# Exact buffer dependencies, earlier loads, and a layer norm spread through the FFN of a transformer block

## The chip, the cores and the metric

The kernel runs on one core of a Trainium2 chip. A core has TensorE (matrix products, with a separate weight load), VectorE, ScalarE and GpSimd, and a sync engine that issues the transfers between HBM and the on-chip memory SBUF. TensorE writes into PSUM, a small memory of eight banks. The metric is the device time of one execution in microseconds (us); lower is better.

## The reference

One pre-norm transformer block on x of 2048 rows by 1024 (bf16), with 32 heads of 32, and an FFN of 3584 hidden columns with the tanh form of GELU:

```python
def _A_ref(x, wqkv, wo):
    qkv = ...                       # (x @ wqkv) split in 3 x 32 heads of 32
    scores = jnp.einsum("bhqd,bhkd->bhqk", q, k) * scale
    p = _softmax(scores, axis=-1)
    o = jnp.einsum("bhqk,bhkd->bhqd", p, v)
    return (...).reshape(B, S, D) @ wo

def _B_ref(x, w1, b1, w2, b2):
    h = _gelu(jnp.einsum("bsd,df->bsf", x, w1) + b1)
    return jnp.einsum("bsf,fd->bsd", h, w2) + b2

h = x + _A_ref(_layernorm(x, axis=-1), A_wqkv, A_wo)
h2 = h + _B_ref(_layernorm(h, axis=-1), B_w1, B_b1, B_w2, B_b2)
```

## The kernel before

**Planner.** The kernel is first written down as a list of tasks for each engine, in program order. Each task names the buffers it reads and writes (`Buf` objects, one per ring slot or bank), and from these the planner derives which semaphore values it must wait for. Each engine then works through its list strictly in order; a wait is issued ahead of the task that needs it (L122). All transfers are issued by the sync engine, also in order (L218), so a transfer whose wait isn't over holds up all later ones.

**Memory.** SBUF and PSUM tensors are allocated like a stack. When a stage ends, its tensors are freed and the next stage's are laid over them. Nothing records which old tensor lies under which new one. So a buffer of a later stage is made by `recycled_buf` (short name `RB`), which lets its first user wait for everything that any engine or transfer lane has been given to do up to then.

**First stage (0 to 247 us).** Layer norm of x, transposes, and the projections to Q, K (transposed) and V, in four chunks of 512 rows.

**Second stage (247 to 1361 us).** Attention. For 4 query chunks x 8 groups of four heads x 16 key tiles, TensorE computes scores (L516), ScalarE the exponentials (L527), TensorE the sums with V (L544) and the denominators (L552). VectorE divides at the end of each group (L563, L564) and writes into OT.

**Third stage (1361 to 1939 us), the one that the change is about.** It works in four chunks (`qc`) of 512 rows, each of four row tiles (`t4`).

- `wo_ln_gen(qc)` is the output projection and the second layer norm. For a row tile it loads the x row tile into `xring3`, makes two accumulation groups of 8 matmuls each (L656) in the PSUM banks `ACC0` onward, copies each out on ScalarE (`attb`, L662) and adds x on VectorE (`hch`, L664). After all four tiles, `ln_batch` takes the statistics of the four (two `bn_stats` a tile, L316, and an aggregate, L318), some small operations on a few columns (L320 to L334, with a square root on ScalarE, L326), then for each tile the subtraction of the mean on ScalarE (L336) and the scaling on VectorE (L339) into `xnb3`. Then each tile is transposed in 8 matmuls (L344) through the one bank `TPB` and copied out on ScalarE into `hnT` (L347).
- `ffn1_gen(qc)` makes the hidden layer in 28 slices (`fc`) of 128 columns, 4 slices for each of 7 blocks of w1 (1 MB each, ring of 3, `w1st`). A slice is 8 matmuls (L701) into one of `NH1P` banks starting at `H1P0`, then the scale and bias on ScalarE (`xh`, L706), two operations on VectorE (`sqf` L709, `uu` L711), and, one slice later, tanh on ScalarE (`th`, L685) and the final product on VectorE (`gT`, L687). `xh`, `sqf`, `uu` and `th` have three slots each.
- `ffn2_plan(qc)` loops over the 28 slices, loads a 256 KB row block of w2 (ring of 4) for each, and adds 8 matmuls (L731), one into each of the eight banks; then come the bias (L737), the residual add on VectorE (`ost`, ring of 4, L746) and the store.

`ffn1_gen` and `wo_ln_gen` are generators. The main loop runs the projection of chunk 0 first. Then, for each chunk, it runs `ffn1_gen(qc)` and after every second slice one step of `wo_ln_gen(qc + 1)`: so the task lists are interleaved in an order fixed by where `yield` stands. Then `ffn2_plan(qc)` follows, which needs all eight banks.

The banks of the third stage before: 0 to 3 for the projection, 4 to 6 for the hidden layer, 7 for the transposes.

Of the kernel before, what the change touches and what calls it, by code (L numbers as in the profile page):

```python
# [6 lines left out]
dt = mybir.dt  # L7
# [43 lines left out]
class Plan:  # L51
    def __init__(self):
        self.tasks = {}
        self.main_flow = {}
        self.all_flows = []

# [4 lines left out]
    def recycled_buf(self):  # L61
        b = Buf()
        for f in self.all_flows:
            hz = f.horizon()
            if hz > 0:
                b.r[f] = hz
        return b
# [61 lines left out]
class LNTemps:  # L129

    def __init__(self, nc, T, pfx, nslots, nbn, mkbuf, tiles=4):
        tq = tiles
        self.stats = T(nc.sbuf_tensor(pfx + "stats", [P, nslots, tq, nbn * 6], dt.float32))
        self.mv = T(nc.sbuf_tensor(pfx + "mv", [P, nslots, tq, 2], dt.float32))
        self.mvb = T(nc.sbuf_tensor(pfx + "mvb", [P, nslots, tq, 2], dt.bfloat16))
        self.mvr = T(nc.sbuf_tensor(pfx + "mvr", [P, nslots, tq, 2], dt.float32))
        self.nm = T(nc.sbuf_tensor(pfx + "nm", [P, nslots, tq, 1], dt.float32))
        self.tb = T(nc.sbuf_tensor(pfx + "tb", [P, nslots, tq, 1], dt.bfloat16))
        self.y0 = T(nc.sbuf_tensor(pfx + "y0", [P, nslots, tq, 1], dt.float32))
        self.r0 = T(nc.sbuf_tensor(pfx + "r0", [P, nslots, tq, 1], dt.float32))  # L140
        self.q0 = T(nc.sbuf_tensor(pfx + "q0", [P, nslots, tq, 1], dt.float32))
        self.y1 = T(nc.sbuf_tensor(pfx + "y1", [P, nslots, tq, 1], dt.float32))
        self.denb = T(nc.sbuf_tensor(pfx + "denb", [P, nslots, tq, 1], dt.bfloat16))
        self.rden = T(nc.sbuf_tensor(pfx + "rden", [P, nslots, tq, 1], dt.float32))
        self.B = [mkbuf() for _ in range(nslots)]
# [15 lines left out]
def build_kernel(nc, A_x, A_wqkv, A_wo, B_w1, B_b1, B_w2, B_b2, out):  # L161
# [23 lines left out]
    with es:  # L185
# [19 lines left out]
        RB = plan.recycled_buf  # L205
# [28 lines left out]
        ident = T(nc.sbuf_tensor("ident", [P, P], dt.bfloat16))  # L234
        ones_pp = T(nc.sbuf_tensor("ones_pp", [P, P], dt.bfloat16))
        ones32 = T(nc.sbuf_tensor("ones32", [P, 32], dt.bfloat16))
        row1 = T(nc.sbuf_tensor("row1", [1, P], dt.bfloat16))
        b2row = T(nc.sbuf_tensor("b2row", [1, D], dt.bfloat16))
        b1col_bf = T(nc.sbuf_tensor("b1col_bf", [P, FC], dt.bfloat16))
        b1half = T(nc.sbuf_tensor("b1half", [P, FC], dt.float32))  # L240
        B_ident, B_ones_pp, B_ones32, B_row1, B_b2row, B_b1bf, B_b1half = (Buf() for _ in range(7))
# [12 lines left out]
        OT = T(nc.sbuf_tensor("OT", [P, NCH, G, 512], dt.bfloat16))  # L254
        B_OT = [[Buf() for _ in range(G)] for _ in range(NCH)]
# [4 lines left out]
        QT = T2(nc.sbuf_tensor("QT", [P, G, S], dt.bfloat16))  # L260
        KT = T2(nc.sbuf_tensor("KT", [P, G, S], dt.bfloat16))
        Vsb = T2(nc.sbuf_tensor("Vsb", [P, NT, D], dt.bfloat16))
        biasm = T2(nc.sbuf_tensor("biasm", [P, G, NCH], dt.float32))
        A2 = T2(nc.sbuf_tensor("A2", [P, G, NCH], dt.float32))
        B2 = T2(nc.sbuf_tensor("B2", [P, G], dt.float32))
        B_QT = [[Buf() for _ in range(NCH)] for _ in range(G)]
        B_KT = [[Buf() for _ in range(NCH)] for _ in range(G)]
        B_V = [[Buf() for _ in range(NVB)] for _ in range(NT)]
        B_biasm = Buf()
        B_A2 = [[Buf() for _ in range(NCH)] for _ in range(G)]  # L270
        B_B2 = [Buf() for _ in range(G)]
# [5 lines left out]
        xnT = T1(nc.sbuf_tensor("xnT", [P, NXT, DC, 512], dt.bfloat16))  # L277
        B_xnT = [[Buf() for _ in range(4)] for _ in range(NXT)]
        NXR = 8
        xring = T1(nc.sbuf_tensor("xring", [P, NXR, D], dt.bfloat16))  # L280
        B_xring = [Buf() for _ in range(NXR)]
        NLN = 8
        NBN = (D + 511) // 512
        xnb = T1(nc.sbuf_tensor("xnb", [P, NLN, D], dt.bfloat16))
        B_xnb = [Buf() for _ in range(NLN)]
        ln1 = LNTemps(nc, T1, "l1", 2, NBN, Buf)
# [3 lines left out]
        wst = T1(nc.sbuf_tensor("wst", [P, NWS, DC, WBLK], dt.bfloat16))  # L290
        B_wst = [Buf() for _ in range(NWS)]
        sqb = T1(nc.sbuf_tensor("sqb", [P, 2, 512], dt.bfloat16))
        B_sqb = [Buf() for _ in range(2)]
        cm = T1(nc.sbuf_tensor("cm", [P, 1], dt.float32))
        B_cm = Buf()
# [3 lines left out]
        tp = ps1.enter_context(nc.psum_tensor("tp", [P, DC * P], dt.bfloat16))  # L299
        B_tp = Buf()  # L300
        NPQ = 3
        psq = ps1.enter_context(nc.psum_tensor("psq", [P, NPQ, 512], dt.float32))
        B_psq = [Buf() for _ in range(NPQ)]
        pn = ps1.enter_context(nc.psum_tensor("pn", [P, 2, 512], dt.float32))
        B_pn = [Buf() for _ in range(2)]
        psv = ps1.enter_context(nc.psum_tensor("psv", [P, 2, 512], dt.float32))
        B_psv = [Buf() for _ in range(2)]

        def ln_batch(L, slot, xs_list, outs_list):
# [25 lines left out]
            for i, ((x_ap, B_x), (xn_ap, B_xn)) in enumerate(zip(xs_list, outs_list)):  # L335
                act(lambda a, L=L, slot=slot, i=i, xn_ap=xn_ap, x_ap=x_ap: a.activation(  # L336
                    xn_ap, x_ap, ACT.Identity, bias=L.nm[:, slot, i, :], scale=1.0),
                    reads=[B_x, Bl], writes=[B_xn])
                dve(lambda v, L=L, slot=slot, i=i, xn_ap=xn_ap: v.tensor_scalar(xn_ap, xn_ap, L.rden[:, slot, i, :], None, ALU.mult),  # L339
                    reads=[B_xn, Bl], writes=[B_xn])  # L340

# [146 lines left out]
        PT = T2b(nc.sbuf_tensor("PT", [P, NPT, 2, 512], dt.bfloat16))  # L488
        B_PT = [RB() for _ in range(NPT)]
        rdenf = T2b(nc.sbuf_tensor("rdenf", [P, 2, 512], dt.float32))  # L490
        B_rdenf = [RB() for _ in range(2)]
# [3 lines left out]
        sT = ps2.enter_context(nc.psum_tensor("sT", [P, NSTP, 2, 512], dt.float32))  # L495
        B_sT = [RB() for _ in range(NSTP)]
        NOD = 2
        OTp = ps2.enter_context(nc.psum_tensor("OTp", [P, NOD, 512], dt.float32))
        DENp = ps2.enter_context(nc.psum_tensor("DENp", [P, NOD, 512], dt.float32))
        B_OTp = [RB() for _ in range(NOD)]  # L500
        B_DENp = [RB() for _ in range(NOD)]

# [84 lines left out]
        Wo = T3(nc.sbuf_tensor("Wo", [P, G, D], dt.bfloat16))  # L587
        B_Wo = RB()
        dma(Wo[:, :, :], A_wo.rearrange("(g p) d -> p g d", p=P), writes=[B_Wo], lanes=lanes_w)
        NHC = 2  # L590
        hch = T3(nc.sbuf_tensor("hch", [P, NHC, 4, D], dt.bfloat16))
        B_hch = [[RB() for _ in range(4)] for _ in range(NHC)]
        attb = T3(nc.sbuf_tensor("attb", [P, 2, OB], dt.bfloat16))
        B_attb = [RB() for _ in range(2)]
        NHN = 2
        hnT = T3(nc.sbuf_tensor("hnT", [P, NHN, DC, 512], dt.bfloat16))
        B_hnT = [[RB() for _ in range(4)] for _ in range(NHN)]
        gT = T3(nc.sbuf_tensor("gT", [P, FC, 512], dt.bfloat16))
        B_gT = [RB() for _ in range(FC)]
        NXR3 = 4  # L600
        xring3 = T3(nc.sbuf_tensor("xring3", [P, NXR3, D], dt.bfloat16))
        B_xring3 = [RB() for _ in range(NXR3)]
        NLN3 = 4
        xnb3 = T3(nc.sbuf_tensor("xnb3", [P, NLN3, D], dt.bfloat16))
        B_xnb3 = [RB() for _ in range(NLN3)]
        ln3 = LNTemps(nc, T3, "l3", 2, NBN, RB)
# [4 lines left out]
        w1st = T3(nc.sbuf_tensor("w1st", [P, NW1, DC, W1B], dt.bfloat16))  # L611
        B_w1st = [RB() for _ in range(NW1)]
        NW2 = 4
        w2st = T3(nc.sbuf_tensor("w2st", [P, NW2, D], dt.bfloat16))
        B_w2st = [RB() for _ in range(NW2)]
        NGL = 3
        xh = T3(nc.sbuf_tensor("xh", [P, NGL, 512], dt.bfloat16))
        sqf = T3(nc.sbuf_tensor("sqf", [P, NGL, 512], dt.bfloat16))
        uu = T3(nc.sbuf_tensor("uu", [P, NGL, 512], dt.bfloat16))
        th = T3(nc.sbuf_tensor("th", [P, NGL, 512], dt.bfloat16))  # L620
        B_xh = [RB() for _ in range(NGL)]
        B_sqf = [RB() for _ in range(NGL)]
        B_uu = [RB() for _ in range(NGL)]
        B_th = [RB() for _ in range(NGL)]
        NOS = 4
        ost = T3(nc.sbuf_tensor("ost", [P, NOS, OB], dt.bfloat16))
        B_ost = [RB() for _ in range(NOS)]
# [4 lines left out]
        B_pb = [RB() for _ in range(8)]  # L632
        ACC0 = 0
        H1P0 = 4
        NH1P = 3
        TPB = 7
        tp3 = pb[:, TPB, :].bitcast(dt.bfloat16)

# [203 lines left out]
```

## Time and profile before

| | |
|---|---|
| time, median of 4 runs | 1942.8 us (1940.69 to 1944.21) |
| span of the profiled execution | 1939.0 us |
| PE (TensorE matmul) busy | 1734.4 us, 89% |
| ACT (ScalarE) busy | 1345.5 us, 69% |
| DVE (VectorE) busy | 507.0 us, 26% |
| third stage | 1360.8 to 1939.0 us |

How to read it: the names in the profile are PE for TensorE's matmuls, PEld for its weight loads, DVE for VectorE, ACT for ScalarE, SPq for the sync engine's queue of transfers. An entry such as `pb<-hnT,w1st` gives the tile written and the tiles read. What stands in brackets at the end of a line is the engine's idle time just before the instruction and what ended it. The shares are averages over three stages with different limits: the second stage, 1114 us long, is mostly ScalarE's, and the third is TensorE's. Two tensors of the first and third stage, `xring` and `xring3`, have one name in the profile, since digits at the end are left out.

### The profile page before, as it was taken

How to read it: one execution, taken by the hardware profiler on the slowest of the kernel's cores; microseconds unless marked ns; L12 is line 12 of the kernel's file. 1: busy time of each engine (PE TensorE's matmuls, PEld its weight loads, DVE VectorE, ACT ScalarE, POOL GpSimd, SP SyncE). 2: the span in 40 equal slices, each digit the busy share in tenths (PEclk: the TensorE clock that was granted, in tenths of full speed). 3: DMA queues.
4: the chain of work that ended last, by engine and by line, in shares of the span. 5: the costliest groups of instructions: out<-in, count | busy, mean ns of one | idle time of the engine just before them, and what ended most of it. 6: DMA issues, size and time to landing. Idle time of an engine off the chain costs nothing.

```text
span 1939.0 us, 24118 instructions
## 1 busy us (share of the span) xinstructions
PE 1734.4 (89%) x9312; PEld 482.7 (25%) x9312; DVE 507.0 (26%) x849; ACT 1345.5 (69%) x1458; POOL 1.0 (0%) x9
## 2 busy tenths in 40 slices
PE   4889989999999999999999999999479779779798
PEld 2344411111111111111111111111134334334343
DVE  5443500010100101001010010110356156165281
ACT  3433389999999999999999999999246045054060
POOL 0000000000000000000000000000000000000000
PEclk9999955555555555555555555555689889889899
DMA  4343200000000000000000000000422432523534
GB/s 113 129 149 122 95 1 1 1 1 1 1 1 1 1 1 1 1 1 1 1 1 1 1 1 1 1 1 1 152 66 76 147 124 93 171 85 109 156 127 131
DMA packets 84176, 100.13 MB, mean 52 GB/s; under 512 B 7265, under 2 KB 64609, under 8 KB 84066
## 3 DMA queue, kind: packets, MB, share of 16 engines
q1 hardware_dynamic: 84066, 98.59, 16.1%
q8 instruction: 78, 1.28, 0.3%
q14 instruction: 32, 0.26, 0.0%
HBM read 94.38 MB, written 4.19 MB: 51 GB/s over the span
## 4 chain that ended last, share of the span: by engine, by line
PE 61%; ACT 18%; issue 15%; DVE 5%; DMA 2%; ACTq 0%; SPq 0%; DVEq 0%
PE sT L516 15%; ACT PT L527 15%; PE pb L731 10%; PE pb L701 9%; PE OTp L544 7%; PE DENp L552 6%; PE psq L390 6%; PE pb L656 3%; PE psv L435 3%; ACT xnb L336 1%; DVE l3stats L316 1%; DVE ost L746 1%; DMA w1st<-in_B_w_dram 1%; PE pn L410 1%; ACT xnT L347 1%
## 5 line engine op out<-in xcount | busy, mean ns | idle before, releaser
L527 ACT ACTIVATE PT<-sT,biasm 128x1024 bf16<-128x1024 f32 x1024 | 1056.4, 1111 | 54.5 <-PE sT L516 54.5
L516 PE MATMUL sT<-QT,KT 32*128 32x512 bf16 x2048 | 590.2, 602 | 57.8 <-ACT PT L527 57.1
L563 DVE RECIPROCAL rdenf<-DENp 128x512 f32<-128x512 f32 x32 | 107.4, 3357 | 992.7 <-PE DENp L552 992.7
L552 PE MATMUL DENp<-PT,ones 128*32 128x512 bf16 x2048 | 330.6, 634 | 0.0
L544 PE MATMUL OTp<-PT,Vsb 128*32 128x512 bf16 x2048 | 317.2, 608 | 0.4 <-ACT PT L527 0.4
L516 PEld LDWEIGHTS sT<-QT,KT 32*128 32x128 bf16 x2048 | 103.1, 99 | 714.1 <-ACT PT L527 712.9
L706 ACT ACTIVATE xh<-pb,b1half 128x512 bf16<-128x512 f32 x112 | 76.8, 686 | 243.3 <-PE pb L701 243.1
L701 PE MATMUL pb<-hnT,w1st 128*128 128x512 bf16 x896 | 210.9, 396 | 34.3 <-DMA w1st<-in_B_w_dram 33.1
L731 PE MATMUL pb<-w2st,gT 128*128 128x512 bf16 x896 | 194.4, 379 | 0.0
L390 PE MATMUL psq<-xnT,wst 128*128 128x512 bf16 x512 | 129.4, 400 | 4.8 <-ACT xnT L347 2.4
L701 PEld LDWEIGHTS pb<-hnT,w1st 128*128 128x128 bf16 x896 | 90.3, 102 | 147.5 <-DMA w1st<-in_B_w_dram 34.6
L731 PEld LDWEIGHTS pb<-w2st,gT 128*128 128x128 bf16 x896 | 87.5, 98 | 106.2 <-issue 1.2
L544 PEld LDWEIGHTS OTp<-PT,Vsb 128*32 128x32 bf16 x2048 | 57.6, 101 | 224.4 <-issue 223.1
L711 DVE SCALAR_TENSOR_TENSOR uu<-sqf,xh 128x512 bf16<-128x512 bf16 x112 | 77.5, 692 | 3.8
L687 DVE SCALAR_TENSOR_TENSOR gT<-th,xh 128x512 bf16<-128x512 bf16 x112 | 76.6, 684 | 3.5 <-ACT th L685 3.2
L685 ACT ACTIVATE th<-uu 128x512 bf16<-128x512 bf16 x112 | 69.7, 622 | 3.6 <-DVE uu L711 2.8
L656 PE MATMUL pb<-Wo,OT 128*128 128x512 bf16 x256 | 59.0, 386 | 13.0 <-DMA Wo<-in_A_wo_dram 13.0
L390 PEld LDWEIGHTS psq<-xnT,wst 128*128 128x128 bf16 x512 | 52.1, 102 | 71.7 <-issue 17.7
L746 DVE TENSOR_TENSOR ost<-pb,hch 128x512 bf16<-128x512 f32 x32 | 19.9, 682 | 188.2 <-PE pb L737 188.0
L552 PEld LDWEIGHTS DENp<-PT,ones 128*32 128x32 bf16 x2048 | 64.3, 114 | 0.0
L709 DVE TENSOR_TENSOR sqf<-xh 128x512 bf16<-128x512 bf16 x112 | 47.5, 424 | 63.1 <-ACT xh L706 62.9
L435 PE MATMUL psv<-wst,xnT 128*128 128x512 bf16 x256 | 55.9, 379 | 0.0
(66 smaller groups left out, 490.2 us busy)
## 6 DMA issues: line engine op xcount, KB each, us to landing
w1st<-in_B_w_dram SPq DMA_DIRECT2D x28, 1024.0 KB, 5.5
w2st<-in_B_w_dram SPq DMA_DIRECT2D x112, 256.0 KB, 2.6
wst<-in_A_wqkv_dram SPq DMA_DIRECT2D x24, 1024.0 KB, 5.0
xring<-in_A_x_dram SPq DMA_DIRECT2D x32, 256.0 KB, 4.2
out_dram<-ost SPq DMA_DIRECT2D x32, 128.0 KB, 1.7
Wo<-in_A_wo_dram SPq DMA_DIRECT2D x1, 2048.0 KB, 8.3
b2row<-in_B_b_dram SPq DMA_DIRECT2D x1, 2.0 KB
b1col_bf<-in_B_b_dram SPq DMA_DIRECT2D x1, 7.0 KB, 4.6
```

The costliest lines, as they stand in the source:

```text
L390: pe(lambda p, dc=dc, b=b, s=s, cin=cin, xt=xt: p.matmul(psq[:, b, :], wst[:, s, dc, cin:cin + P], xnT[:, xt, dc, :], start=(dc == 0), sto ...
L435: pe(lambda p, dc=dc, t4=t4, s=s, pvs=pvs, xt=xt: p.matmul(psv[:, pvs, 0:OB], xnT[:, xt, dc, t4 * P:(t4 + 1) * P], wst[:, s, dc, :], start ...
L516: pe(lambda p, s=s, j=j, kt=kt, g=g, hl=hl, qc=qc: p.matmul(sT[:, s, j, :], KT[32 * hl:32 * hl + 32, g, kt * P:(kt + 1) * P], QT[32 * hl:3 ...
L527: act(lambda a, s=s, ps=ps, g=g, qc=qc: a.activation(PT[:, ps, :, :], sT[:, s, :, :], ACT.Exp, bias=biasm[:, g, qc:qc + 1], scale=SCALE), ...
L544: pe(lambda p, j=j, kt=kt, g=g, hl=hl, ps=ps, start=start, stop=stop, oi=oi: p.matmul(OTp[32 * hl:32 * hl + 32, oi, :], Vsb[:, kt, g * P + ...
L552: pe(lambda p, j=j, hl=hl, ps=ps, start=start, stop=stop, oi=oi: p.matmul(DENp[32 * hl:32 * hl + 32, oi, :], ones32[:, :], PT[:, ps, j, :] ...
L563: dve(lambda v, rs=rs, oi=oi: v.reciprocal(rdenf[:, rs, :], DENp[:, oi, :]), reads=[B_DENp[oi]], writes=[B_rdenf[rs]])
L656: pe(lambda p, sa=sa, g=g, qc=qc, t4=t4, j=j: p.matmul(pb[:, sa, 0:OB], OT[:, qc, g, t4 * P:(t4 + 1) * P], Wo[:, g, j * OB:(j + 1) * OB], ...
L701: pe(lambda p, hb=hb, s=s, dc=dc, f4=f4, hn=hn: p.matmul(pb[:, hb, :], w1st[:, s, dc, f4 * P:(f4 + 1) * P], hnT[:, hn, dc, :], start=(dc = ...
L706: act(lambda a, gs=gs, hb=hb, fc=fc: a.activation(xh[:, gs, :], pb[:, hb, :], ACT.Identity, bias=b1half[:, fc:fc + 1], scale=0.5), reads=[ ...
L711: dve(lambda v, gs=gs: v.scalar_tensor_tensor(uu[:, gs, :], sqf[:, gs, :], C1, xh[:, gs, :], ALU.add, ALU.mult), reads=[B_sqf[gs], B_xh[gs ...
L731: pe(lambda p, ci=ci, fc=fc, t4=t4, j=j, s2=s2: p.matmul(pb[:, ci, 0:OB], gT[:, fc, t4 * P:(t4 + 1) * P], w2st[:, s2, j * OB:(j + 1) * OB] ...
```

## The change

It has four parts, all in the planning code; the arithmetic is the same.

1. **Exact dependencies.** `recycled_buf` goes. Each tensor is now allocated through `SB` (SBUF) or `PSM` (PSUM), which look up its address and call `track`. That finds all earlier tensors whose bytes or banks overlap with it and lets the new tensor's buffers wait for the last writers and readers of those alone. It is for letting a new stage's loads start before the old stage has ended.
2. **Order in SBUF.** `Wo`, `xring3` and `w1st` are allocated last in the third stage, behind a pad of 17,920 bytes per partition, so that they do not lie over what attention uses last. It is for loading them while attention runs.
3. **The layer norm in pieces.** `ln_batch` is split for the third stage: `ln_stats` follows each row tile's projection, `ln_small` follows the fourth, and the norms and transposes are steps of their own: norm 0, norm 1, transpose 0, norm 2, transpose 1, norm 3, transpose 2, transpose 3. It is for not blocking VectorE and ScalarE in one long burst. `wo_ln_gen` then has 13 steps instead of 9, and FFN1 gives it 14.
4. **Banks and prefetch.** The projection gets 2 banks instead of 4 and the hidden layer 5 instead of 3 (2 to 6), counted from bank 2 anew in each chunk. `ffn2_plan` reads its results out in the order 2, 3, 4, 5, 6, 0, 1, 7, so that the next chunk's hidden layer finds its banks free first. Two blocks of w1 for the next chunk are loaded ahead of `ffn2_plan`'s w2 loads. It is for starting the next chunk's FFN1 right after FFN2.

```diff
-    def recycled_buf(self):
-        b = Buf()
-        for f in self.all_flows:
-            hz = f.horizon()
-            if hz > 0:
-                b.r[f] = hz
-        return b
+    def track(self, space, lo, hi, bufs):
...
+        for (sp, l, h, obufs) in self.regions:
+            if sp == space and l < hi and lo < h:
+                for ob in obufs:
+                    merge(ob.w)
+                    for f, v in ob.r.items():
+                        merge((f, v))
+        for b in bufs:
+            for f, v in deps.items():
+                if b.r.get(f, 0) < v:
+                    b.r[f] = v
+        self.regions.append((space, lo, hi, bufs))
...
-        Wo = T3(nc.sbuf_tensor("Wo", [P, G, D], dt.bfloat16))
-        B_Wo = RB()
-        dma(Wo[:, :, :], A_wo.rearrange("(g p) d -> p g d", p=P), writes=[B_Wo], lanes=lanes_w)
...
+        ost, B_ost = SB(T3, "ost", [P, NOS, OB], dt.bfloat16, NOS)
+        T3(nc.sbuf_tensor("pad", [P, 17920 // 2], dt.bfloat16))
+        Wo, B_Wo = SB(T3, "Wo", [P, G, D], dt.bfloat16)
+        dma(Wo[:, :, :], A_wo.rearrange("(g p) d -> p g d", p=P), writes=[B_Wo], lanes=lanes_w)
+        xring3, B_xring3 = SB(T3, "xring3", [P, NXR3, D], dt.bfloat16, NXR3)
+        w1st, B_w1st = SB(T3, "w1st", [P, NW1, DC, W1B], dt.bfloat16, NW1)
...
-        H1P0 = 4
-        NH1P = 3
+        NACC = 2
+        H1P0 = 2
+        NH1P = 5
...
-                    sa = ACC0 + (t4 * NVB + j) % 4
+                    sa = ACC0 + (t4 * NVB + j) % NACC
...
-                xs_list.append((hch[:, hs, t4, :], B_hch[hs][t4]))
-                ls = tt % NLN3
-                outs_list.append((xnb3[:, ls, :], B_xnb3[ls]))
+                ln_stats(ln3, qc % 2, t4, hch[:, hs, t4, :], B_hch[hs][t4])
                 yield
-            ln_batch(ln3, qc % 2, xs_list, outs_list)
+            ln_small(ln3, qc % 2, 4)
             yield
...
+            for step, t4 in ((nrm, 0), (nrm, 1), (trn, 0), (nrm, 2), (trn, 1), (nrm, 3), (trn, 2), (trn, 3)):
+                step(t4)
                 yield
...
+        def prefetch_w1(qc, nblk):
+            for blk in range(nblk):
+                w1_prefetched[(qc, blk)] = load_w1(qc, blk)
...
-                    hb = H1P0 + h1count % NH1P
+                    hb = H1P0 + (h1count - h1base) % NH1P
...
-            for ci, (t4, j) in enumerate(combos):
+            for ci in [2, 3, 4, 5, 6, 0, 1, 7]:
+                t4, j = combos[ci]
...
+            if qc + 1 < NCH:
+                prefetch_w1(qc + 1, NW1 - 1)
             ffn2_plan(qc)
```

## The prediction

> **What bounds the kernel now.** I read the page's forty slices first, then the chain that ended last between 1360 and 1939 us, then the timeline of one chunk (1535 to 1635 us), and then the waits of the DMA queue.
>
> ```profile
> PE   4889989999999999999999999999479779779798
> PEclk9999955555555555555555555555689889889899
> ```
>
> TensorE is full until slice 28, at half clock while attention runs there, paced by ScalarE's exponentials (1024 of 1.11 us). The holes lie after it, from 1361 us on: the third stage (output projection, layer norm, FFN). Nothing in the diff reaches attention except its buffers' first waits. The chain of the third stage shows its holes; columns are start us, us, what.
>
> ```profile
> 1360.86 3.37 DVE rdenf L563
> 1364.25 0.70 DVE OT L564
> 1365.47 8.27 DMA Wo<-in_A_wo_dram
> 1373.83 15.59 PE pb L656 x64
> ...
> 1410.08 1.03 ACT hnT L347
> 1411.24 5.28 PE pb L701 x16
> 1416.53 3.45 PE pb L656 x16
> ...
> 1538.56 1.84 PE pb L737 x8
> 1540.43 2.50 DVE ost L746 x4
> ...
> 1545.84 5.43 DMA w1st<-in_B_w_dram
> 1551.32 5.23 PE pb L701 x16
> 1556.55 3.45 PE pb L656 x16
> ```
>
> The reader is to see three things. From 1360.8 (end of attention's last matmul) to 1411.24 TensorE does only 64 matmuls and 32 transposes. From 1540.40 to 1551.32 it waits for w1, whose load is issued only at 1545.84. And 16 matmuls take 3.45 us when the chain is dense (0.216 us each) but 5.23 after a hole. The timeline of the chunk shows a fourth hole:
>
> ```profile
> 1580.56 7.07 PE L701 MATMUL pb<-hnT,w1st 128*128 128x512 bf16 x32
> 1586.61 1.42 DVE L316 BATCH_NORM_STATS2 l3stats<-hch 128x6 f32<-128x512 bf16 x2
> 1594.22 0.20 ACT L326 ACTIVATE l3y<-l3tb 128x4 f32<-128x4 bf16 x1 [7.50 <-DVE l3tb L324]
> 1597.21 1.03 PE L344 MATMUL pb<-ident,xnb 128*128 128x128 bf16 x8 [9.57 <-DVE xnb L339]
> 1606.55 0.42 DVE L709 TENSOR_TENSOR sqf<-xh 128x512 bf16<-128x512 bf16 x1
> 1608.21 0.42 DVE L709 TENSOR_TENSOR sqf<-xh 128x512 bf16<-128x512 bf16 x1
> ```
>
> VectorE runs the statistics of all four row tiles as one burst from 1586.61, ScalarE sits in front of the square root for 7.5 us, no h1 bank is emptied, and TensorE stands 9.57 us. The two L709 starts, 1.66 us apart, are VectorE's pace when it has work queued: one hidden slice costs it 1.66 us and TensorE 8 x 0.216 = 1.73. The waits of the DMA queue (us in total, times, longest) say why loads come late:
>
> ```profile
> SPq L122 <- DVE OT L564: 1128.6, 1, 1128.6
> SPq L218 <- DVE ost L746: 41.9, 32, 9.1
> ```
>
> The queue stood 1128.6 us in front of Wo, until VectorE's last attention product; and w1 of a new chunk stands behind output stores that wait for the adds of L746.
>
> **What the Trainium skill says.** "TensorE: Matmul & The Clock Gate", Part 1: an idle TensorE falls to half clock and wakes after about 3.4 us of activity; the trace agrees (0.43 us a matmul for the first eight after 1373.83, 0.216 later). The same page and part: ScalarE and VectorE take instructions strictly in order; the burst at 1586.61 with the GELU behind it agrees. "ScalarE: Activation LUTs", What ACT_TABLE_LOAD costs: some 1283 ns for the load; here 1.28 us at 1585.44. "PSUM — Partial Sum Buffer", Specifications: eight banks of 2 KiB; the stage has used all eight, split 4 (projection), 3 (h1), 1 (transposes), and the change resplits them 2, 5, 1.
>
> **Part 1: exact dependencies, and Wo, xring3 and w1st moved up.** Before, every third-stage buffer waits for all work so far. After, each waits for the users of the bytes or banks it overlaps. Do the three overlap attention's? Bytes per partition, counted from the end of OT: attention holds QT, KT, Vsb (3 x 32,768), three small tensors (288), PT (12,288), rdenf (4,096): up to 114,976. In front of Wo now stand hch 16,384, attb 2,048, hnT 16,384, gT 28,672, xnb3 8,192, LN temporaries 800 (tensors of 16 bytes taken as 32), w2st 8,192, GELU 12,288, ost 4,096 and the pad 17,920: 114,976. They meet exactly, so Wo, four x rows and one w1 block can load during attention, its DMA being idle. The next x row in the queue still waits for chunk 0's first add.
>
> TensorE then goes from attention's last matmul straight into the projection. I keep its measured 15.6 us, half-clock start included. The statistics of a tile now follow its adds (a tile gives VectorE 0.85 + 1.70 us, TensorE 3.45), so after the last group remain copy and add 1.1, one tile's statistics 1.7 (1392.11 to 1393.81), the ten small operations 2.1 (1397.20 to 1399.28), and norms with transposes. The latter took 12.0 (1399.28 to 1411.24); two norms, transpose, then alternating, start the first hnT copy 1.3 us earlier: 11.0. Sum 15.6 + 1.1 + 1.7 + 2.1 + 11.0 = 31.5 against 50.4: **-18.9**. At attention's start nothing is won: the first exponential waits for its table load behind the last V copy, as before.
>
> **Part 2: layer norm spread through the chunk.** Chunk 1 takes 1551.32 to 1630.08 = 78.8 us; the other two with a projection are alike. TensorE's own work is (224 + 64) x 0.2157 + 4 x 0.45 = 63.9. In the projection part, a period of two slices and one tile costs TensorE 6.91 and VectorE 2 x 1.66 + 0.9 + 1.7 = 5.9, so the statistics fit in its idle time and even work off the adds of the previous chunk. Call T the end of the fourth tile. From there VectorE has statistics to T + 2.95, then 20 slices x 1.66 = 33.2, small operations 2.1, four scalings 4 x 0.54 = 2.2, and about 1 us of holes at the two table loads. It ends near T + 42; the product that frees the xh slot of slice 27 (three slots) comes some 4 us earlier, T + 38, and xh of slice 27 at T + 38.8. TensorE by itself ends at T + 36.3, reaching that bank 0.9 later at T + 37.2, where the second matmul needs it. So 1.6 us of the lag shows; with a short wait of the last transpose I take 2. Five h1 banks instead of three hide the rest, since TensorE may run five slices ahead of ScalarE. The Sqrt still holds ScalarE, but only for a few small operations. Chunk: 65.9. Savings: chunk 0, which still starts at half clock (1.8), 11.1; chunks 1 and 2, 12.9 each; last chunk 1.7, as its first 16 matmuls are no longer slow. Sum **-38.6**. Two projection banks suffice: a group takes 1.73 us, its copy 0.6 plus 0.2 of wait.
>
> **Part 3: w1 prefetched and banks read in h1's order.** Two blocks of w1 for the next chunk are issued before w2. Each waits for its slot's last reader, block 4 or 5 of seven, so behind it on the queue stand the w2 loads, and TensorE's second matmul waits for those. Block 5 ends at T + 29.2; the 1 MB lands 5.5 later, and 256 KB of w2 a little behind it, at about T + 36, before T + 38. I cost it at zero. At the boundary, TensorE needs only bank 2, first to be read: one L746 of 0.7 us plus 0.1. Three boundaries took 10.9, 11.1 and 11.1; 33.1 - 3 x 0.8 = **-30.7**. The other adds run beside the first slices: bank 0 comes sixth, 3.8 us in, and the projection asks for it 4.2 us in.
>
> **Sum.** 18.9 + 38.6 + 30.7 = 88.2; 1942.8 - 88.2 = 1854.6, about **1855 us**.
>
> **Rivals.**
> 1. VectorE's lag shows more. It is nearly TensorE's equal in FFN1 (1.66 against 1.73), and ScalarE with a norm or an hnT copy in every second slice is near it too: 2 x (0.59 + 0.62) + 1.05 = 3.5 per 3.45. If each of three chunks loses 5 us instead of 2: 1864. For it: the narrow margin. Against: after the burst at 1606 to 1630, VectorE caught up with TensorE never stopping.
> 2. w2 comes late behind the prefetch. If it queues its full time behind 1 MB, w2 begins near T + 38, and three later tiles follow close: 4 us in three chunks, 1867. Against: w2 took 2.6 us each and TensorE uses one per 1.73.
> 3. Wo isn't early, because an overlap remains (the regions meet to the byte). Then its 13.0 us come back: 1868.
> 4. Slower: with its holes gone, TensorE is held at a lower clock. Its 465 us of dense work in this stage at 0.80 would cost 116: 1971. For it: attention runs at half clock though 95% busy. Against: the window below, wholly busy, at 1.00 (columns: us, busy of PE, PEld, DVE, ACT, POOL, clock, DMA share, GB/s).
>
> ```profile
> 1630.00:1680.00 50.00, 50.00 (x233) 22.38 (x231) 3.25 (x6) 1.83 (x3) 0.00 (x0) 1.00 0.42 126
> ```
>
> **How the numbers follow.** Forecast 0.62, rivals 1 to 4: 0.20, 0.10, 0.06, 0.02. The unknown costs are the residual per chunk (0 to 5 us, so -6 to +9 on the sum), the boundary (0.8 to 2, +4) and the startup's half clock (0 to 3, about 2 either way). Low end 1855 - 6 - 3 = 1846; high end takes in rivals 1 to 3 singly: 1870. Any one of the three parts alone makes it faster by far over 0.2%: faster 0.97, same 0.01, slower 0.02.
>
> **What would show it.** Right: Wo's load far before 1361 and the first projection matmul within 1 us of attention's last; L316 in four separate places per chunk and no hole over 3 us before a transpose; FFN1 of the next chunk starting 0.8 us after L737 with 3.45 us for its first 16 matmuls; a third stage near 490 us instead of 578. Wrong: TensorE waiting for w2 when FFN2 starts, for ScalarE's bank reads over 3 us per chunk, for Wo, or a granted clock under 1.00 in dense windows.

## The result, and the profile after

The changed kernel takes 1851.4 us (median of 8 runs, 1848.3 to 1852.8) against 1941.5 us of the kernel before on the same chips (12 runs): a ratio of 0.9534, 95% interval 0.9524 to 0.9543. The forecast was 1855 us, with a range of 1846 to 1870.

The forty slices of the page after:

```profile
PE   4899889999999999999999999999979999999998
PEclk9999965555555555555555555555569999999999
```

The holes at the end of the row for PE are gone but for the first slice of the third stage, and the clock row stands at 9 from slice 30 on (counted from 0), where it was 8 or 9 before. The chain that ended last, in the same columns as before (L717, L782, L812, L818 and L828 are the former L656, L701, L731, L737 and L746):

```profile
1359.02 15.52 PE pb L717 x64
...
1390.05 5.02 PE pb L782 x16
1395.07 3.45 PE pb L717 x16
...
1504.87 1.84 PE pb L818 x8
1506.73 0.70 DVE ost L828
1507.57 3.61 PE pb L782 x16
1511.18 3.45 PE pb L717 x16
...
1622.85 1.30 DVE ost L828 x2
1624.17 3.70 DMA out_dram<-ost
1627.96 0.70 DVE ost L828
1628.71 3.63 PE pb L717 x16
...
1741.39 50.02 PE pb L782 x224
```

The projection starts at 1359.02, where attention ends; FFN1 starts at 1390.05 (before: 50.4 us after attention, now 31.0). At the first boundary one add, 0.70 us, stands between FFN2 and the next FFN1, and 16 matmuls take 3.61 us. Two lines were not foreseen: at the second boundary the chain goes through a store (1624.17), and in the last chunk 224 matmuls take 50.02 us, not the 48.3 of full clock. Where the loads went is in the timeline of the DMA queue and, in the second fence, in its waits:

```profile
231.41 0.42 SPq L276 DMA_DIRECT2D Wo<-in_A_wo_dram  x1
231.87 11.09 SPq L276 DMA_DIRECT2D xring<-in_A_x_dram  x4
246.32 0.38 SPq L276 DMA_DIRECT2D w1st<-in_B_w_dram  x1
```

```profile
SPq L276 <- DVE hch L725: 1127.2, 4, 1118.5
```

Wo, four row tiles of x and one block of w1 are issued between 231 and 246 us, as attention begins, and the fifth row tile waits 1118.5 us for the first add of the third stage, as the prediction said. The layer norm of chunk 1 in the timeline of the changed kernel:

```profile
1399.65 1.42 DVE L387 BATCH_NORM_STATS2 l3stats<-hch 128x6 f32<-128x512 bf16 x2
1406.55 1.42 DVE L387 BATCH_NORM_STATS2 l3stats<-hch 128x6 f32<-128x512 bf16 x2
1413.46 1.42 DVE L387 BATCH_NORM_STATS2 l3stats<-hch 128x6 f32<-128x512 bf16 x2
1420.37 1.42 DVE L387 BATCH_NORM_STATS2 l3stats<-hch 128x6 f32<-128x512 bf16 x2
1426.04 0.20 ACT L400 ACTIVATE l3y<-l3tb 128x4 f32<-128x4 bf16 x1 [0.80 <-DVE l3tb L398]
1429.76 1.14 ACT L412 ACTIVATE xnb<-hch,l3nm 128x1024 bf16<-128x1024 bf16 x1
1432.89 0.61 PE L420 MATMUL pb<-ident,xnb 128*128 128x128 bf16 x8
```

Four pairs of statistics lie 6.9 us apart, one to a row tile; the square root holds ScalarE 0.80 us instead of 7.50; the first transpose follows 3 us behind its norm and its line shows no idle time in front.

Where the 90 us of the profiled spans (1939.0 and 1849.0) came from, measured between the first or last matmuls of each section (us):

| section | before | after | saved | forecast |
|---|---|---|---|---|
| end of attention (from the span's start) | 1360.8 | 1359.0 | 1.8 | 0 |
| attention's end to FFN1 of chunk 0 | 50.4 | 31.0 | 19.4 | 18.9 |
| FFN1 of chunks 0, 1, 2 | 78.6, 78.6, 78.5 | 66.1, 64.7, 66.2 | 12.6, 13.9, 12.3 | 11.1, 12.9, 12.9 |
| FFN1 of chunk 3 | 49.9 | 49.9 | 0.0 | 1.7 |
| three boundaries | 10.9, 11.1, 11.1 | 0.87 each | 30.5 | 30.7 |

FFN2 grew by 0.6 us in all, and the end of the kernel stayed. The 1.8 us of the first row are scatter: in the twelve traces of the versions told of below, whose first two stages are the same, attention ended anywhere between 1358.5 and 1361.9 us.

### The profile page after: what moved, and what is told of

Same layout as the page of the kernel before. It is cut to its first block, busy times and chain, and to the rows that moved or that the text cites. A ratio compares the mean times of both kernels' runs of the same rounds, so it can differ in the third digit from the quotient of the medians.

```text
span 1849.0 us, 24060 instructions
## 1 busy us (share of the span) xinstructions
PE 1748.6 (95%) x9312; PEld 479.7 (26%) x9312; DVE 500.7 (27%) x849; ACT 1370.8 (74%) x1458; POOL 1.0 (0%) x9
## 4 chain that ended last, share of the span: by engine, by line
PE 60%; ACT 18%; issue 15%; DVE 5%; DMA 1%; ACTq 0%; SPq 0%; DVEq 0%
PE sT L587 16%; ACT PT L598 16%; PE pb L812 10%; PE OTp L615 8%; PE pb L782 7%; PE DENp L623 6%; PE psq L466 6%; PE pb L717 3%; PE psv L511 3%; DVE uu L792 1%; DVE gT L771 1%; PE pn L486 1%; DVE sqf L790 1%; ACT xnb L376 1%; ACT xnT L423 1%
## 5 line engine op out<-in xcount | busy, mean ns | idle before, releaser
L598 ACT ACTIVATE PT<-sT,biasm 128x1024 bf16<-128x1024 f32 x1024 | 1083.3, 1111 | 26.4 <-PE sT L587 1.6
L587 PE MATMUL sT<-QT,KT 32*128 32x512 bf16 x2048 | 618.2, 602 | 29.9 <-ACT PT L598 4.8
L787 ACT ACTIVATE xh<-pb,b1half 128x512 bf16<-128x512 f32 x112 | 76.4, 682 | 192.5 <-PE pb L782 192.5
L782 PE MATMUL pb<-hnT,w1st 128*128 128x512 bf16 x896 | 200.9, 383 | 3.8 <-DVE ost L828 2.6
L812 PE MATMUL pb<-w2st,gT 128*128 128x512 bf16 x896 | 194.7, 379 | 0.3
L782 PEld LDWEIGHTS pb<-hnT,w1st 128*128 128x128 bf16 x896 | 87.6, 99 | 109.6 <-issue 5.4
L812 PEld LDWEIGHTS pb<-w2st,gT 128*128 128x128 bf16 x896 | 87.4, 98 | 106.9 <-issue 2.1
L828 DVE TENSOR_TENSOR ost<-pb,hch 128x512 bf16<-128x512 f32 x32 | 20.0, 683 | 188.7 <-PE pb L818 186.6
L717 PE MATMUL pb<-Wo,OT 128*128 128x512 bf16 x256 | 59.0, 386 | 1.4 <-DVE ost L828 1.4
L478 ACT ACTIVATE QT<-psq 128x512 bf16<-128x512 f32 x32 | 19.1, 597 | 43.1 <-PE psq L466 43.1
```

The source lines that it names most:

```text
L587: pe(lambda p, s=s, j=j, kt=kt, g=g, hl=hl, qc=qc: p.matmul(sT[:, s, j, :], KT[32 * hl:32 * hl + 32, g, kt * P:(kt + 1) * P], QT[32 * hl:3 ...
L598: act(lambda a, s=s, ps=ps, g=g, qc=qc: a.activation(PT[:, ps, :, :], sT[:, s, :, :], ACT.Exp, bias=biasm[:, g, qc:qc + 1], scale=SCALE), ...
L717: pe(lambda p, sa=sa, g=g, qc=qc, t4=t4, j=j: p.matmul(pb[:, sa, 0:OB], OT[:, qc, g, t4 * P:(t4 + 1) * P], Wo[:, g, j * OB:(j + 1) * OB], ...
L782: pe(lambda p, hb=hb, s=s, dc=dc, f4=f4, hn=hn: p.matmul(pb[:, hb, :], w1st[:, s, dc, f4 * P:(f4 + 1) * P], hnT[:, hn, dc, :], start=(dc = ...
L812: pe(lambda p, ci=ci, fc=fc, t4=t4, j=j, s2=s2: p.matmul(pb[:, ci, 0:OB], gT[:, fc, t4 * P:(t4 + 1) * P], w2st[:, s2, j * OB:(j + 1) * OB] ...
```

## The experiments

Each is an edit of the changed kernel; ratios are to the kernel before, with their 95% interval. "FFN1" is the time from its first matmul to FFN2's first in the profiled execution.

### Wo's place, 32 bytes lower

```diff
-        T3(nc.sbuf_tensor("pad", [P, 17920 // 2], dt.bfloat16))
+        T3(nc.sbuf_tensor("pad", [P, 17888 // 2], dt.bfloat16))
```

> The changed kernel with the pad 32 bytes shorter, so that Wo overlaps the last 32 bytes of rdenf. My theory: the early load is worth the whole wait for Wo; Wo's load then starts only after the last attention product (L635) and the first projection matmul comes about 13 us after attention's last matmul instead of at once: 1851.4 + 13 = 1864 us. Rival: the start of the stage is bound by the chain of layer norm 0 anyway and the load hides behind it: 1851 to 1854 us.

Measured: 1865.8 us, ratio 0.9599 (0.9583 to 0.9615). The chain of this kernel at the start of the third stage:

```profile
1366.12 8.75 DMA Wo<-in_A_wo_dram
1374.92 15.75 PE pb L717 x64
```

Attention's last matmul ended at 1361.76, the projection began at 1374.92: a hole of 13.2 us, and the time is 14.4 us above the changed kernel's. The rival falls. Thirty-two bytes of overlap cost the whole early load, since the queue stops at Wo (1133.1 us, until VectorE's last attention product) and everything behind it waits too.

### No prefetch of w1

```diff
-                prefetch_w1(qc + 1, NW1 - 1)
+                prefetch_w1(qc + 1, 0)
```

> The changed kernel without the two w1 blocks loaded ahead of FFN2; bank order and all else stay. My theory: w1 of the next chunk goes back behind the eight stores, three boundaries grow from 0.87 to about 11 us, and two of the three next chunks start at half clock again (1.7 each): +30 to +34, 1881 to 1886 us. Rival: the bank order alone frees TensorE and the load comes nearly in time: under 1857 us.

Measured: 1886.4 us, ratio 0.9709 (0.9694 to 0.9723). The chain at the first boundary:

```profile
1509.50 2.49 DVE ost L828 x4
1514.91 5.61 DMA w1st<-in_B_w_dram
1520.57 5.99 PE pb L782 x16
```

The three holes are 11.1 us each, and the matmuls behind all three start slow. So 35.1 us are lost, 1 us more than the upper end of what was expected: 3 x (11.1 - 0.87) = 30.7 of them are the holes themselves. The bank order without the prefetch is worth nothing, as w1's transfer ends last and the holes are as long as in the kernel before.

### The burst, and where the transposes stand

Three kernels separate the two things that part 3 of the change does: spreading the statistics, and moving the transposes away from the norms. The first puts everything back into one burst, with the transposes right behind:

```diff
+                yield
+            for t4 in range(4):
                 ln_stats(ln3, qc % 2, t4, hch[:, hs, t4, :], B_hch[hs][t4])
-                yield
             ln_small(ln3, qc % 2, 4)
-            yield
...
-            for step, t4 in ((nrm, 0), (nrm, 1), (trn, 0), (nrm, 2), (trn, 1), (nrm, 3), (trn, 2), (trn, 3)):
-                step(t4)
+            for t4 in range(4):
+                nrm(t4)
+            yield
+            for t4 in range(4):
+                trn(t4)
                 yield
```

> The changed kernel with the layer norm of a chunk as one burst after the fourth tile (four statistics, small operations, four norms), and the transposes in the steps right behind it, as in the kernel before. Five h1 banks, prefetch and early loads stay. My theory: each of three chunks loses again what it lost before (FFN1 about 77 to 79 us instead of 65 to 66), and the startup loses the 5 us of three tiles' statistics: 1851.4 + 3 x 11 + 5 = about 1889 us. Rival: five h1 banks instead of three were what closed the hole, and the burst costs little with them: under 1865 us.

Measured: 1898.1 us (4 runs, 1894.9 to 1920.4), ratio 0.9794 (0.9738 to 0.9850). FFN1 takes 79.8, 79.4 and 78.6 us: the old length, with five banks. Each of them includes about 1.6 us of a slow start. The rival falls; the loss is larger than the theory's, 12 to 15 us a chunk and 5.3 at the startup.

The second keeps the burst but leaves the transposes at their late steps (the edit is shown against the first):

```diff
             for t4 in range(4):
                 nrm(t4)
             yield
-            for t4 in range(4):
-                trn(t4)
-                yield
+            for t4 in (None, None, 0, None, 1, None, 2, 3):
+                if t4 is not None:
+                    trn(t4)
+                yield
```

> The same single burst of statistics, small operations and norms after the fourth tile, but the transposes at the late steps where the changed kernel has them (steps 16, 20, 24, 26 of FFN1). Theory of the prediction: the burst itself costs, since three tiles' statistics (5.1 us) no longer lie in VectorE's idle time and its lag comes out where FFN2 needs the last h1 banks: about 5 us in each of three chunks and 5 at the startup, 1872 us. Rival: TensorE only stood because the first transpose stood too early in its order; with the transposes late the burst is hidden and only the startup loses its 5 us: 1857 us.

Measured: 1889.4 us, ratio 0.9726 (0.9712 to 0.9741); FFN1 76.8, 75.0 and 76.2 us. Neither figure was right: the burst costs 10 us a chunk. Its timeline during FFN1 of chunk 0 (L786 and L791 are the changed kernel's L782 and L787):

```profile
1432.24 1.41 DVE L387 BATCH_NORM_STATS2 l3stats<-hch 128x6 f32<-128x512 bf16 x2
1439.85 0.21 ACT L400 ACTIVATE l3y<-l3tb 128x4 f32<-128x4 bf16 x1 [7.49 <-DVE l3tb L398]
1441.11 4.26 ACT L412 ACTIVATE xnb<-hch,l3nm 128x1024 bf16<-128x1024 bf16 x4 [1.05 <-DVE l3rden L408]
1445.28 0.66 ACT L791 ACTIVATE xh<-pb,b1half 128x512 bf16<-128x512 f32 x1
1446.00 3.60 PE L786 MATMUL pb<-hnT,w1st 128*128 128x512 bf16 x8 [7.55 <-ACT xh L791]
```

The burst does not lag on VectorE alone: ScalarE stands 7.49 us in front of the square root and then does four norms in a row, so it reads no h1 bank from 1431.1 (the table load) to 1445.28. TensorE fills its five banks and stops for 7.55 us, and the line names the xh that frees the bank. Afterwards it starts at half clock (8 matmuls in 3.60 us).

The third spreads the statistics but ties each norm to its transpose, at the early steps:

```diff
-            for step, t4 in ((nrm, 0), (nrm, 1), (trn, 0), (nrm, 2), (trn, 1), (nrm, 3), (trn, 2), (trn, 3)):
-                step(t4)
-                yield
+            for t4 in range(4):
+                nrm(t4)
+                trn(t4)
+                yield
```

> The changed kernel with the statistics still spread over the tiles, but each norm and its transpose together in one step, in steps 12, 14, 16 and 18 of FFN1, where the kernel before had its transposes. With the burst, moving the transposes late had brought FFN1 of a chunk only from about 78.6 to 75.5 us. Theory: the burst of statistics was nearly all of the hole, so FFN1 stays under 68 us even with early transposes: under 1862 us. Rival: both are needed, since the first norm ends about 13 us after the fourth tile and TensorE reaches the early transpose 7 us after it: about 71 us a chunk, 1870 us.

Measured: 1913.5 us, ratio 0.9854 (0.9834 to 0.9873), the slowest of all, and far from both figures; FFN1 87.2, 85.9 and 82.4 us. The timeline shows a round trip that neither theory had:

```profile
1434.86 1.14 ACT L412 ACTIVATE xnb<-hch,l3nm 128x1024 bf16<-128x1024 bf16 x1
1436.71 1.03 PE L420 MATMUL pb<-ident,xnb 128*128 128x128 bf16 x8 [5.46 <-DVE xnb L415]
1437.78 1.02 ACT L423 ACTIVATE hnT<-pb 128x1024 bf16<-128x1024 bf16 x1 [1.78 <-PE pb L420]
1440.50 0.69 ACT L788 ACTIVATE xh<-pb,b1half 128x512 bf16<-128x512 f32 x1 [1.70 <-PE pb L783]
1443.33 1.14 ACT L412 ACTIVATE xnb<-hch,l3nm 128x1024 bf16<-128x1024 bf16 x1
1445.15 0.62 PE L420 MATMUL pb<-ident,xnb 128*128 128x128 bf16 x8 [2.96 <-DVE xnb L415]
```

The norm stands in ScalarE's order behind the xh of the two slices that TensorE has just finished. So TensorE always meets its transpose before the norm is done, and waits (5.46, then 2.96 us); ScalarE then waits for the transpose (1.78) and, after it, for the next slice (1.70). This repeats for each of the four. Put together, the statistics spread and the transposes late give 64.7 us; either alone gives 75 or more. In the changed kernel one or two other steps stand between a norm and its transpose, here none does. This run also has the transposes earlier; no run keeps the distance at the early steps, so the two are not told apart by times, and it is the waits above that point to the distance.

### Three h1 banks

```diff
-        H1P0 = 2
-        NH1P = 5
+        H1P0 = 4
+        NH1P = 3
...
-            for ci in [2, 3, 4, 5, 6, 0, 1, 7]:
+            for ci in [4, 5, 6, 0, 1, 2, 3, 7]:
```

> The changed kernel with three h1 banks (4 to 6) instead of five, read out first after FFN2; banks 2 and 3 are unused outside FFN2. Theory of the prediction: five banks hide VectorE's lag, so with three TensorE waits for a bank in the second half of FFN1: about 3 us a chunk, 1860 us. Rival: the lag shows only at FFN2's start, where the last bank has to be read whatever the number of banks, and three slots of xh bind as before: within 2 us of 1851 us.

Measured: 1851.8 us, ratio 0.9531 (0.9518 to 0.9544); FFN1 takes 66.0, 66.4, 66.1 and 48.3 us, the first three of them with a slow start of some 1.6 us, which leaves about the changed kernel's 64.7. The rival holds: with the burst gone, three banks are as good as five.

### The bias of FFN2: first, and twice

```diff
+            for ci, (t4, j) in enumerate(combos):
+                pe(lambda p, ci=ci, j=j: p.matmul(pb[:, ci, 0:OB], row1[:, :], b2row[:, j * OB:(j + 1) * OB],
+                                                    start=True, stop=False),
+                   reads=[B_row1, B_b2row, B_pb[ci]], writes=[B_pb[ci]], inc=(ci == len(combos) - 1))
             for fc in range(FC):
...
-                        start=(fc == 0), stop=False),
+                        start=False, stop=(fc == FC - 1)),
...
-            for ci, (t4, j) in enumerate(combos):
-                pe(lambda p, ci=ci, j=j: p.matmul(pb[:, ci, 0:OB], row1[:, :], b2row[:, j * OB:(j + 1) * OB],
-                                                    start=False, stop=True),
-                   reads=[B_row1, B_b2row], writes=[], inc=(ci == len(combos) - 1))
```

> The changed kernel with the eight bias matmuls of FFN2 (one row each) moved from the end of FFN2 to its start. In the changed kernel's trace the first matmuls after the third boundary ran at half clock for about 3.4 us (0.43 us each) though TensorE had stood only 0.9 us, and at the first two boundaries they did not. Theory: the one-row matmuls count as nearly idle, so that 1.7 us of them and the 0.9 us hole together can drop the clock; with full matmuls in front of the hole no boundary is slow: 16 matmuls in about 3.6 us at all three, 1849.5 us. Rival: the hole alone can do it, by chance: one of three boundaries or so still slow, 1851 us.

> A second look at the kernel with the bias matmuls moved to FFN2's start. Theory: again no boundary is slow (64.7, 64.7 and 48.4 us of FFN1 after the three boundaries). Rival: one or two of the three are slow.

The kernel that issues the bias twice, still at the end:

```diff
-            for ci, (t4, j) in enumerate(combos):
-                pe(lambda p, ci=ci, j=j: p.matmul(pb[:, ci, 0:OB], row1[:, :], b2row[:, j * OB:(j + 1) * OB],
-                                                    start=False, stop=True),
+            for rep in range(2):
+                for ci, (t4, j) in enumerate(combos):
+                    pe(lambda p, ci=ci, j=j, rep=rep: p.matmul(pb[:, ci, 0:OB], row1[:, :], b2row[:, j * OB:(j + 1) * OB],
+                                                        start=False, stop=(rep == 1)),
...
```

> The changed kernel with the eight one-row bias matmuls at FFN2's end issued twice (the bias is added twice, so the output has one b2 too many). Costs 1.7 us in each of four chunks by itself. Theory: 3.5 us of one-row matmuls and the 0.87 us hole drop the clock at all three boundaries, so FFN1 takes 66.3 us and 50.0 us instead of 64.7 and 48.35. Rival: the one-row matmuls count as busy, and the slow start stays a matter of chance, at about one boundary in two.

The first 3.4 us after each of the three boundaries, in the changed kernel (columns: stretch, us, busy of PE, PEld, DVE, ACT, POOL, granted clock, DMA share, GB/s):

```profile
1507.57:1510.97 3.40, 3.40 (x16) 1.55 (x17) 3.34 (x6) 0.69 (x1) 0.00 (x0) 1.00 0.49 166
1623.69:1627.09 3.40, 3.40 (x16) 1.46 (x16) 2.33 (x4) 0.69 (x1) 0.00 (x0) 1.00 0.37 117
1741.39:1744.79 3.40, 3.40 (x9) 1.24 (x10) 3.35 (x6) 0.00 (x0) 0.00 (x0) 0.54 0.49 166
```

and in the kernel with the bias twice:

```profile
1512.17:1515.57 3.40, 3.40 (x9) 1.24 (x10) 3.36 (x6) 0.00 (x0) 0.00 (x0) 0.54 0.50 168
1631.53:1634.93 3.40, 3.40 (x9) 1.23 (x10) 2.33 (x4) 0.00 (x0) 0.00 (x0) 0.53 0.37 119
1750.93:1754.33 3.40, 3.40 (x9) 1.21 (x10) 3.37 (x6) 0.00 (x0) 0.00 (x0) 0.52 0.50 169
```

and in the second trace with the bias first:

```profile
1508.57:1511.97 3.40, 3.40 (x16) 1.54 (x17) 3.35 (x6) 0.69 (x1) 0.00 (x0) 1.00 0.50 168
1624.68:1628.08 3.40, 3.40 (x16) 1.46 (x16) 2.33 (x4) 0.69 (x1) 0.00 (x0) 1.00 0.36 117
1742.52:1745.92 3.40, 3.40 (x16) 1.56 (x17) 3.36 (x6) 0.69 (x1) 0.00 (x0) 1.00 0.50 168
```

The slow stretches shown have nine matmuls instead of 16, at a clock of 0.52 to 0.54. The hole in front is 0.87 or 0.88 us in all nine. Counted over the traces of all versions with this hole: with the bias last, 9 of 21 boundaries were slow, at a clock of 0.50 to 0.69 (the changed kernel, the 32 bytes, both burst kernels, the joined norms, three banks and eight slots); with the bias twice, 3 of 3; with the bias first, 0 of 6, the clock 1.00 in each. If the boundaries were independent, six fast ones in a row would come about once in 29 at a rate of 9 in 21 (an estimate from these counts). So the one-row matmuls very probably belong to the cause: a hole of 0.87 us alone was never seen to do it. The theory holds, as far as 30 boundaries can tell. In the second trace one FFN1 took 66.5 us, but its clock was 1.00: there the projection waited 1.6 us for a store.

The times of the version with the bias first, 1849.8 us (ratio 0.9522, 0.9509 to 0.9536) and 1850.7 us in the single run of the second, are too close to 1851.4 to show the gain by themselves. With the bias twice a single run took 1862.1 us; of the 10.7 us more, 4 x 1.7 = 6.9 are the added matmuls.

### Output slots, and banks released one by one

Eight slots for the output instead of four:

```diff
-        NOS = 4
+        NOS = 8
...
-        T3(nc.sbuf_tensor("pad", [P, 17920 // 2], dt.bfloat16))
+        T3(nc.sbuf_tensor("pad", [P, 13824 // 2], dt.bfloat16))
```

> The changed kernel with eight output slots instead of four (the pad shrinks by the same bytes, so Wo keeps its place). In the changed kernel's trace the sixth add at the second boundary waited 1.9 us for a store and TensorE's first projection group 1.4 us for that add's bank. Theory: that wait goes, 1 to 2 us in those executions that have it: 1850 us. Rival: nothing visible, 1851 us, as it is rare.

Measured: 1851.2 us, ratio 0.9529 (0.9516 to 0.9542): no difference that the times show. In its trace no add waits for a store, and FFN1 is 64.7 us after the first and second boundary. The wait itself isn't rare: most versions with four slots show it at one boundary, where VectorE waits 1.3 to 2.4 us, of which up to 1.8 reach TensorE.

The bias first, and the last slice of FFN2 in the order in which the banks are needed, each signalled on its own (shown against the version with the bias first):

```diff
-                for ci, (t4, j) in enumerate(combos):
+                for ci in ([2, 3, 4, 5, 6, 0, 1, 7] if fc == FC - 1 else range(8)):
+                    t4, j = combos[ci]
...
-                        writes=[], inc=(ci == len(combos) - 1))
-            for ci in range(len(combos)):
-                B_pb[ci].w = (fpe, fpe.value())
+                        writes=[], inc=(fc == FC - 1 or ci == len(combos) - 1))
+                    if fc == FC - 1:
+                        B_pb[ci].w = (fpe, fpe.value())
```

> As the one before, and the last slice of FFN2 goes through the banks in the order 2, 3, 4, 5, 6, 0, 1, 7 and signals each bank on its own, so that VectorE's adds begin while TensorE still works on the other banks. Theory: the hole of 0.87 us at three boundaries goes (2.6), no boundary is slow (1.7), and the end of the kernel is 1.5 us shorter, as the last eight adds start 1.5 us before TensorE's end: about 1845.6 us. Rival: the adds are held by the four store slots or the stores' completion sets the end: 1849 us.

Measured: 1846.5 us, ratio 0.9501 (0.9488 to 0.9514). The hole at the three boundaries is gone: FFN1's first matmul follows without a gap, at full clock (FFN1 takes 64.8, 64.8 and 48.4 us after them). From TensorE's end to the span's end it takes 5.8 us (1838.8 to 1844.6), against 7.2 in the changed kernel, as the theory said. Now the released banks and the eight slots together:

> Bias first, each bank released on its own in the last slice, and eight output slots. With four slots this kernel's last adds waited 3.5 us for stores at the third boundary and again at the end of the kernel, where TensorE had ended at 1838.84 us and the span at 1844.6. Theory: with eight slots the end needs only the rest of the adds and the last store, about 1.5 us less than with four: 1845 us. Rival: the last store's completion sets the end in any case: 1846.5 us.

Measured: 1843.5 us (5 runs, 1843.1 to 1845.4), ratio 0.9490 (0.9477 to 0.9503): below the changed kernel's interval, so this version beats both the kernel before and the changed kernel. What the eight slots add to the released banks is not shown. The theory's 1.5 us at the end did not come: from TensorE's end to the span's end it takes 5.6 us (1835.5 to 1841.1), against 5.8 with four slots. The trace with four slots has one wait for a store, 2.26 us at the third boundary, and none over 0.1 us at the end, unlike what the expectation says. Of the 3.5 us between the two profiled spans (1844.6 and 1841.1), 3.1 lie ahead of attention's end, where the two kernels are alike.

## Why the prediction was right, step by step

On the profiled spans the changed sections save 88.8 us, FFN2 takes 0.6 back, and the 88.2 us that remain are the forecast sum to the tenth. The third stage took 490.0 us, as forecast. That the sum fits so well is luck, for terms of Part 2 miss both ways and cancel.

**Part 1** was right in mechanism and size: 19.4 us against 18.9. That Wo lies clear of rdenf, by less than 32 bytes, and that the lost load is worth 13 us, the pad of 32 bytes less shows. The tail of norms and transposes took 10.6 us (1379.43 to 1390.05) where 11.0 was said.

**Part 2** has the right sum, 38.9 against 38.6, out of terms that are off. The residual per chunk, 2 us, was too large: a chunk without other trouble takes 64.7 us against 63.9 of TensorE's own work, so 0.8. In that chunk TensorE never waits for an h1 bank, so the 1.6 us forecast for VectorE's lag did not come; the only wait is 0.55 us in front of the last transpose, for which 0.4 had been allowed. In return chunk 2 lost 1.4 us behind the add that waits for a store: the step "bank 0 comes sixth, 3.8 us in" forgot that the sixth add needs one of four output slots. And the 1.7 us of the last chunk did not come, since its start was slow after a hole of 0.87 us.

The step that five h1 banks hide the lag was wrong: three do as well. On the burst, the reading of the trace was right: ScalarE stands in front of the square root and no h1 bank is emptied. With the transposes late this still holds, for 14 us. But the cost worked out for a chunk has VectorE's lag alone; for the late burst 5 us a chunk were expected from it, and 10 were measured. And with the statistics spread but the transposes tied to their norms at the early steps a chunk takes 82 to 87 us, more than with the burst. The prediction worked out that distance for the startup only; in the chunks it allowed for no more than a short wait of the last transpose.

**Part 3** was right: 30.5 us against 30.7, and without the prefetch 35 us come back. In the changed kernel no matmul waited for w2 behind the prefetch (0.3 us of idle time in front of all 896 matmuls of FFN2).

**The rivals.** VectorE's lag did not show, w2 was not late, Wo was early, and the clock in dense stretches stayed at 1.00 (1750 to 1792 us, for one).

## What to carry to other kernels

Work in a queue that runs strictly in order must be placed by when its inputs are ready. Here one or two steps of other work between a norm on ScalarE and its transpose on TensorE were enough; with none, the two engines took turns in waiting. When a ring of buffers is laid over an earlier stage, its neighbours decide when the stage can start loading; an overlap of 32 bytes per partition was enough to lose it. And when a long hole is closed, look at what small things now stand behind it: here eight one-row matmuls and the release of all eight banks at once, together 5 us of 1851 (1846.5 us without them).

## What the runs showed of the hardware

A hole of 0.87 us on TensorE was followed by half clock for some 3 us in 9 of 21 cases when 1.7 us of one-row matmuls stood in front of it, in 3 of 3 with 3.5 us of them, and in 0 of 6 with full matmuls there. The Trainium skill, "TensorE: Matmul & The Clock Gate", Part 1, states that the clock falls after an idle window of about 3.4 us, and that this window doesn't start with the kernel. The holes here are much shorter than that, so the page's rule alone does not foresee the slow starts. That a one-row matmul counts as little activity would explain them, and the free-running window why they come at some boundaries and not at others; the runs show the granted clock, not what the chip counts.
